# Decode attention over 65,536 keys: the first piece of keys issued in two halves of partitions, by SyncE and by ScalarE

## The chip, the core and the metric

The kernel runs on one core of a Trainium2 chip. The metric is the device time of one execution in microseconds; lower is better. Engines are called PE (TensorE), DVE (VectorE), ACT (ScalarE), POOL (GpSimd) and SP (SyncE). SP and ACT can issue transfers; each has a queue of its own (q1 for SP, q10 for ACT in the profile), and both feed the same 16 DMA engines.

## The reference

One query token attends over a long cache, with 32 query heads and 8 key/value heads, all in bfloat16:

```python
B, Hq, Hkv, Sq, Sk, D = 1, 32, 8, 1, 65536, 128
k = jnp.repeat(k, rep, axis=1)          # rep = Hq // Hkv = 4
v = jnp.repeat(v, rep, axis=1)
scores = jnp.einsum("bhqd,bhkd->bhqk", q, k) * D ** -0.5
p = softmax(scores, axis=-1)
return jnp.einsum("bhqk,bhkd->bhqd", p, v)
```

The keys and the values of one key/value head are 16.8 MB each, so 268.4 MB are read in all; the output is 8 KB.

## The kernel before

**Tiling.** There are G = 8 groups (one key/value head with its H = 4 query heads). A group's 65,536 keys are laid out as 128 partitions with 512 keys each (`kr[g]`, `vr[g]`), and handled in two halves of NT = 256 keys per partition. Such a half is a tile: 128 partitions x 64 KiB, 8.4 MB. `buf` holds three tiles, used in a ring. A piece of a tile is loaded by `load(at, src, s, lo, n)` (L134), always for all 128 partitions, from `lo` for `n` keys.

**Order of transfers.** SP issues every load of keys and values, in a fixed order `tiles`: both key tiles of group 0, then of group 1, then values and keys of later groups in turn. The first four loads are half tiles of keys (128 partitions x 32 KiB, 4.2 MB); the first of them is issued as SP's very first instruction, ahead of the barrier that opens the program (`tc.close()`, `tc.compile()`, L147 in the profile), the other three right behind that barrier, and then the first tile of group 1. From then on, SP waits before each load until the tile three places earlier has been used up: for keys on `clr` (the bank clears of the scores) or `kb`, for values on `vit`. The last value tile is cut into eight `PIECES`, the smallest at the end, so that little work is left when the last bytes arrive.

**Semaphores of the keys.** `sK[b][x]` counts the landing of half x in ring place b, by 16 for each load. `take` waits for a count and takes it off again.

**Work of the engines.** DVE first builds small selection matrices, waits for q on `sQ` and transposes it (L310). q (32 x 256 bytes) is ACT's first transfer (L227), issued behind the barrier. Then DVE loops over the groups, in blocks with branches (`keys`, `keys0`, `keys1`, `keys2`, `turned`). `turn(b)` takes `sK[b][x]` for both halves of a tile and transposes the keys in place (L320). PE takes `kt` and multiplies the turned keys into `sc`, one bank for each half tile (`bank`, `scores`, L465). ACT does the exponentials (L244), DVE the maxima and the transposes of the weights, and PE accumulates the weighted values of the group before into `psum_o` (`values`, L489). Between PE's query product (L446) and the first scores, ACT casts the spread query into `qx` (L229) and POOL multiplies it into the sliding weights `wq` (L208).

**The tail.** For the last value tile, PE waits for the pieces one by one (L542, L554), DVE picks from `psum_o` (L333), ACT scales and stores. In DVE's block `last`, a few `nop` instructions count up `dl`, ahead of `dve.wait_ge(vdone, 2)` and behind it.

At the end POOL clears all semaphores in `cleared`, which is the list of those allocated up to that line.

Of the kernel before, what the change touches and what calls it, by code (L numbers as in the profile page):

```python
# [15 lines left out]
P = 128  # L16
D = 128
NT = 256
# [14 lines left out]
def kernel(  # L33
# [18 lines left out]
    _, Hkv, Sk, _ = k.shape  # L52
# [5 lines left out]
    pe, dve, act, pool, sp = nc.tensor, nc.vector, nc.scalar, nc.gpsimd, nc.sync  # L58
    half = NT * D
    ring = 3 * half  # L60

    def sbuf(name, shape, dtype=fp32):
        return nc.alloc_sbuf_tensor(name, list(shape), dtype)
# [4 lines left out]
    buf = sbuf("buf", (P, ring), bf16)  # L68
# [27 lines left out]
    def sem(name):  # L96
        sems.append(nc.alloc_semaphore(name))
        return sems[-1]

    sK = [[sem(f"sK{b}{x}") for x in range(2)] for b in range(3)]  # L100
    sC, sD = sem("sC"), sem("sD")
    sL = [sem(f"sL{x}") for x in range(sum(map(len, BY.values())))]
    sP = [sem(f"sP{x}") for x in range(len(PIECES))]
    sQ = sem("sQ")
    sV = sem("sV")
    kt = sem("kt")
    clr = sem("clr")
# [21 lines left out]
    kr = [k[0, g].rearrange("(p n) d -> p (n d)", p=P) for g in range(G)]  # L129
    vr = [v[0, g].rearrange("(p n) d -> p (n d)", p=P) for g in range(G)]  # L130

    def load(at, src, s, lo=0, n=NT):
        at = at % 3 * half + lo * D
        return sp.dma_start(  # L134
            out=buf[:, at:at + n * D], in_=src[:, s * half + lo * D:s * half + (lo + n) * D]
        )

    first = load(0, kr[0], 0, 0, NT // 2)  # L140
    tc.no_tile_sem_insts.add(first.ins.name)
    first.then_inc(sK[0][0], 16)
    tc.add_to_no_dep_group("first", first.ins)
    tc.declare_fence(pool.nop().ins, group="first")
    home = nc.cur_bb.parent
    tc.close()
# [11 lines left out]
    for at, (kind, h, s) in enumerate(tiles):  # L158
# [35 lines left out]
        out=ident[:, :], in_=ident[:, :], compare_op=ALU.not_equal, fill=1.0,  # L194
# [8 lines left out]
    for g in range(G):  # L203
        if g == 0:
            pool.wait_ge(qxs, 1)
        else:
            pool.wait_ge(outs, g)
        pool.tensor_tensor(  # L208
            out=wv[:, :, :, 0:H],
# [12 lines left out]
    def take(engine, semaphore, n=1):  # L222
# [7 lines left out]
        out=qx[:, :].rearrange("p (b r h) -> p b h r", b=2, r=2),  # L230
        in_=misc[:, 0:P].rearrange("p (b h r) -> p b h r", b=2, r=2),
# [9 lines left out]
    for g in range(G + 1):  # L241
        if g < G:
            act.wait_ge(nms, g + 1)
            act.activation(  # L244
                out=E[:, :], in_=sc[:, :], func=ACT.Exp, bias=nmb[:, 0:1], scale=SCALE,
# [4 lines left out]
        at = max(g - 1, 0) * D  # L250
        act.activation(  # L251
            out=o_out[:, at:at + D], in_=psum_f[0:H, 0:D], func=ACT.Copy, scale=rl
# [12 lines left out]
        out=o_out[:, 0:D], in_=misc[0:H, 0:D], func=ACT.Copy, scale=rl_next  # L265
# [5 lines left out]
    def value(reg, below):  # L271
        return bass.RuntimeValue.of_register_unchecked(reg, min_val=0, max_val=below - 1)

    def moved(ap, by):

        return bass.AP(ap.tensor, ap.offset + by, ap.ap)
# [7 lines left out]
    def select(out, pattern, **at):  # L284
# [7 lines left out]
        out=rep.rearrange("p (a x) -> p a x", a=4),  # L292
        in_=ident[0:32, 0:32].unsqueeze(1).broadcast_to([32, 4, 32]),
# [6 lines left out]
        out=rows4[:, :].rearrange("k (y d) -> k y d", y=4),  # L300
        in_=ident[0:4, 0:4].unsqueeze(2).broadcast_to([4, 4, D]),
# [3 lines left out]
        out=away.rearrange("k (q z r h) -> k z q r h", q=4, z=2, r=4)[:, 0],  # L305
# [5 lines left out]
        out=qt.bitcast(fp32), in_=qn.bitcast(fp32)  # L311
# [10 lines left out]
    def weights(s):  # L322

        at = slice(1024 * s, 1024 * (s + 1))
        return dve.transpose(out=Ew[:, at], in_=E[:, at])  # L325

    def next_over():

        return dve.tensor_copy(out=rl, in_=rl_next)  # L329

    def picked():

        return dve.tensor_reduce(  # L333
            out=o_r[:, 0:D], in_=psum_o[:, :].rearrange("p (y d) -> p d y", y=4), axis=AX.X, op=ALU.max
        )

    def over():

        dve.reciprocal(out=rl_next, in_=psum_f[0:H, D:D + 1]).then_inc(rls, 1)  # L339
# [6 lines left out]
    r_h, r_k = dve.alloc_register("h"), dve.alloc_register("k")  # L346
    h, kb_at = value(r_h, G + 1), value(r_k, 3)
    dve.reg_mov(r_h, 0)
    dve.br("keys")

    with block("keys"):
# [15 lines left out]
    with block("turned"):  # L367
# [8 lines left out]
            out=same[:, :].rearrange("p (x h) -> p x h", h=H),  # L376
# [11 lines left out]
    with block("last"):  # L388
        dve.wait_ge(exd, 1)
        dve.wait_ge(vit, NT // STEP * (2 * G - 3))  # L390
        weights(0)
        dve.wait_ge(vdone, 1)
        next_over().then_inc(mxs, 1)
        picked().then_inc(mxs, 1)
        weights(1).then_inc(sP[0], 16)
        dve.wait_ge(pes, 2)
        over()


        for _ in range(6):  # L400
            dve.nop().then_inc(dl, 1)
        dve.wait_ge(vdone, 2)
        picked().then_inc(mxs, 1)
        for _ in range(5):
            dve.nop().then_inc(dl, 1)
        dve.nop().then_inc(fin, 1)
        dve.br("done")
# [22 lines left out]
    def column(row):  # L430

        return 4 * (row // W * W + W - 1 - row % W)
# [26 lines left out]
    with block("scores"):  # L459
# [3 lines left out]
        for y in range(4 * N):  # L463
            m, n = y % 4, y // 4
            pe.matmul(  # L465
                out=bank,
# [17 lines left out]
    with block("values"):  # L484
        take(pe, sV)
        weight = value(r_w, 2048 - 127)
        rows = value(r_p, ring - STEP * D + 1)
        for j in range(STEP // 4):
            last = pe.matmul(  # L489
                out=psum_o[0:16, :], lhsT=moved(Ew[:, column(4 * j + 3):][:, 0:16], weight),  # L490
# [14 lines left out]
    with block("summed"):  # L505
# [4 lines left out]
            out=misc[:, :], lhsT=same[:, :], rhs=each[:, :].unsqueeze(1).broadcast_to([P, 16, 32]),  # L510
# [22 lines left out]
    with block("tail"):  # L533
        at = sum(PIECES[:MOVED])
# [3 lines left out]
        for n, land in left[:1]:  # L538
            pe.wait_ge(land, 16)
            for row in range(at, at + n, 4):  # L540
                qd = row // 4 % 4 * 32
                pe.matmul(  # L542
                    out=psum_o[qd:qd + 16, :], lhsT=Ew[:, final + column(row + 3):][:, 0:16],
# [4 lines left out]
        for y, (n, land) in enumerate(left[1:]):  # L548
# [4 lines left out]
            for row in range(at, at + n):  # L553
                last = pe.matmul(  # L554
                    out=misc[0:H, 0:D], lhsT=Ew[:, final + column(row):][:, 0:H],
# [43 lines left out]
```

## Time and profile before

| what | value |
|---|---|
| median of 3 runs | 627.47 us (627.43 to 627.98) |
| the profiled execution | 628.09 us |
| its span, first to last instruction | 626.2 us |
| granted TensorE clock, mean | 0.926 |
| bytes read | 268.44 MB, 429 GB/s over the span |
| busy: PE, DVE, ACT, POOL | 80%, 53%, 3%, 1% |
| time of q1's packets, share of 16 DMA engines | 99.4% |
| first key load issued | 0.73 us |
| DVE's first turn of keys | 12.88 us |

How to read it: times in the profile are microseconds from the start of the span. A busy share says how much of the span an engine worked. A DMA share of 1.0 in a stretch means that all 16 DMA engines had a packet under way all the time; a packet is counted where it starts, so in short stretches the share and the GB/s swing above and below. A name like `SPq` or `DVEq` is the engine's own sequencer: waits and issues that are not compute. In a line of the stretches, the columns are the stretch, its length, busy time of PE, PEld, DVE, ACT and POOL with the number of instructions, the granted clock, the DMA share and GB/s.

### The profile page before, as it was taken

The page shows a single profiled execution, that of the slowest core. Times are in us where ns is not written, and L with a number is a line of the kernel's source. Part 1 is how long each engine was busy: PE and PEld are TensorE (multiplying, and loading weights), DVE is VectorE, ACT ScalarE, POOL GpSimd, SP SyncE. Part 2 cuts the span into 40 slices and gives each one's busy share as a digit, 9 for nine tenths or more (in the row PEclk, how much of TensorE's full clock was granted, in tenths as well). Part 3 has the DMA queues.
Part 4 walks back from the last instruction along what each step waited for, and adds up shares of the span by engine and source line. Part 5 has one row for each costly group of instructions (what it writes and reads, how often), then busy time and mean ns, then how long its engine had stood idle before and what let it go on. Part 6 is the DMA issues. An engine that isn't in the chain of part 4 may idle for free. (4 is left out here: it accounts for less than half of the span.)

```text
span 626.2 us, 8002 instructions
## 1 busy us (share of the span) xinstructions
PE 501.8 (80%) x2186; PEld 203.8 (33%) x2186; DVE 331.1 (53%) x109; ACT 21.1 (3%) x28; POOL 6.0 (1%) x16
## 2 busy tenths in 40 slices
PE   0587398798995879948799397993979939899998
PEld 0233043243331333313333133331433314333433
DVE  4984894689213892148921488215872169621010
ACT  1000100100010000100001000010000100001000
POOL 2000000000000000000000000000000000000000
PEclk9989599798998789987999779997889978999999
DMA  9999999999999999999999999999999999999998
GB/s 371 435 467 402 419 452 402 469 402 469 402 469 402 469 402 469 402 469 402 469 402 460 410 427 444 402 469 402 469 402 469 402 435 435 469 402 433 425 415 336
DMA packets 6425, 268.46 MB, mean 429 GB/s; under 512 B 792, under 2 KB 1048, under 8 KB 1176
## 3 DMA queue, kind: packets, MB, share of 16 engines
q1 hardware_dynamic: 6336, 268.44, 99.4%
q10 hardware_dynamic: 88, 0.02, 0.0%
q14 instruction: 1, 0.01, 0.0%
HBM read 268.44 MB, written 0.01 MB: 429 GB/s over the span
## 5 line engine op out<-in xcount | busy, mean ns | idle before, releaser
L320 DVE STREAM_TRANSPOSE buf<-buf 128x8192 f32<-128x8192 f32 x32 | 276.9, 8691 | 95.9 <-DVEq L224 95.9
L465 PE MATMUL sc<-buf,zeros 128*128 x1024 | 247.6, 401 | 0.0
L489 PE MATMUL psum_o<-buf,Ew 128*16 x1008 | 224.0, 380 | 6.6 <-PEq L224 6.6
L465 PEld LDWEIGHTS sc<-buf,zeros 128*128 x1024 | 102.3, 100 | 137.4 <-issue 39.1
L489 PEld LDWEIGHTS psum_o<-buf,Ew 128*16 x1008 | 88.8, 88 | 138.1 <-issue 48.5
L423 PE MATMUL sc<-zeros 128*128 128x512 bf16 x32 | 14.0, 439 | 96.5 <-PEq L224 96.5
L333 DVE TENSOR_REDUCE o_r<-psum_o 128x128 f32<-128x512 f32 x10 | 6.9, 688 | 94.6 <-DVEq L224 69.1
L329 DVE COPY o_r<-o_r 4x1 f32<-4x1 f32 x9 | 1.3, 142 | 77.2 <-DVEq L224 64.2
L423 PEld LDWEIGHTS sc<-zeros 128*128 128x128 bf16 x32 | 3.1, 98 | 105.6 <-issue 104.4
L244 ACT ACTIVATE zeros<-sc,nmb 128x2048 bf16<-128x2048 f32 x8 | 15.7, 1967 | 539.8 <-DVE nmb L384 539.8
L325 DVE STREAM_TRANSPOSE Ew<-zeros 128x1024 bf16<-128x1024 bf16 x18 | 22.3, 1239 | 13.8 <-PE psum_o L489 13.8
L509 PE MATMUL misc<-each,same 128*128 128x512 f32 x18 | 11.4, 720 | 8.3 <-PEq L224 8.3
L372 DVE TENSOR_REDUCE mx<-sc 128x1 f32<-128x2048 f32 x8 | 18.0, 2252 | 0.0
L446 PE MATMUL misc<-Ew 32*128 32x128 bf16 x1 | 0.3, 283 | 10.6 <-DVE Ew L310 10.6
L208 POOL TENSOR_TENSOR zeros<-qx,quad 128x64 bf16<-128x64 bf16 x8 | 2.3, 292 | 486.8 <-ACT o_out L251 480.7
L509 PEld LDWEIGHTS misc<-each,same 128*128 128x128 f32 x18 | 2.9, 201 | 8.6 <-issue 8.5
L426 PE MATMUL sc<-zeros 128*128 128x1 bf16 x32 | 5.2, 163 | 0.0
L423 PE MATMUL psum_o<-rows,zeros 4*128 4x512 bf16 x10 | 4.5, 452 | 0.0
L291 DVE CAST Ew<-ident 32x128 bf16<-32x128 f32 x1 | 3.0, 2984 | 2.7 <-POOL ident L193 2.7
L426 PEld LDWEIGHTS sc<-zeros 128*128 128x128 bf16 x32 | 3.0, 95 | 3.9
L251 ACT ACTIVATE o_out<-psum_f,o_r 4x128 bf16<-4x128 f32 x9 | 3.1, 344 | 27.9 <-DVE o_r L339 27.9
L436 PE MATMUL psum_f<-o_r,sel 128*4 128x129 f32 x18 | 3.9, 302 | 0.0
(32 smaller groups left out, 32.0 us busy)
## 6 DMA issues: line engine op xcount, KB each, us to landing
buf<-in_k_dram SPq DMA_DIRECT2D x6, 4096.0 KB, 28.4
buf<-in_v_dram SPq DMA_DIRECT2D x4, 4096.0 KB, 31.8
buf<-in_v_dram SPq DMA_DIRECT2D x2, 2048.0 KB, 30.0
buf<-in_v_dram SPq DMA_DIRECT2D x2, 1024.0 KB, 35.2
buf<-in_v_dram SPq DMA_DIRECT2D x1, 1408.0 KB, 39.2
buf<-in_v_dram SPq DMA_DIRECT2D x1, 288.0 KB, 39.4
buf<-in_v_dram SPq DMA_DIRECT2D x1, 224.0 KB, 39.6
buf<-in_k_dram SPq DMA_DIRECT2D x13, 32.5
```

Source lines behind the costliest of these rows:

```text
L244: act.activation(out=E[:, :], in_=sc[:, :], func=ACT.Exp, bias=nmb[:, 0:1], scale=SCALE, accum_out=o_r[:, D:D + 1],).then_inc(exd, 1)
L251: act.activation(out=o_out[:, at:at + D], in_=psum_f[0:H, 0:D], func=ACT.Copy, scale=rl).then_inc(outs, 1)
L320: dve.transpose(out=kv, in_=kv).then_inc(kt, 1)
L325: return dve.transpose(out=Ew[:, at], in_=E[:, at])
L333: return dve.tensor_reduce(out=o_r[:, 0:D], in_=psum_o[:, :].rearrange("p (y d) -> p d y", y=4), axis=AX.X, op=ALU.max)
L372: after(dve.tensor_reduce(out=mx[:, :], in_=sc[:, :], axis=AX.X, op=ALU.max))
L423: return pe.matmul(out=bank, lhsT=lhsT, rhs=rhs, start=True, stop=False)
L426: return pe.matmul(out=bank[:, 0:1], lhsT=zer[:, 0:P], rhs=zer[:, 0:1], start=False, stop=True)
L436: return pe.matmul(out=out[0:H, 0:n], lhsT=sel[:, :], rhs=o_r[:, 0:n], start=start, stop=stop)
L465: pe.matmul(out=bank, lhsT=moved(wq[:, m * SLIDE + 4 * n:][:, 0:P], slide), rhs=moved(T[:, n, m // 2, m % 2], keys), start=False, stop=False,)
L489: last = pe.matmul(out=psum_o[0:16, :], lhsT=moved(Ew[:, column(4 * j + 3):][:, 0:16], weight), rhs=moved(buf[:, 4 * j * D:][:, 0:4 * D], ...
L509: pe.matmul(out=misc[:, :], lhsT=same[:, :], rhs=each[:, :].unsqueeze(1).broadcast_to([P, 16, 32]), start=True, stop=True,).then_inc(pes, 1)
```

## The change

The first half tile of keys is no longer one transfer of 128 partitions issued by SP. SP issues partitions 0 to 63 of it and ACT partitions 64 to 127, each as the first instruction of its engine, ahead of the barrier. SP's half counts on `sK[0][0]` as before, ACT's on a new semaphore `sF`. DVE waits for `sF` once, behind the transpose of q and before the loop over the groups. One `nop` of DVE in the block `last` is dropped. ACT's transfer of q now stands behind ACT's half of the keys in q10. All other transfers are issued as before.

```diff
-    sQ = sem("sQ")
+    sQ, sF = sem("sQ"), sem("sF")
...
-    first = load(0, kr[0], 0, 0, NT // 2)
-    tc.no_tile_sem_insts.add(first.ins.name)
-    first.then_inc(sK[0][0], 16)
-    tc.add_to_no_dep_group("first", first.ins)
+    for engine, at, land in ((sp, 0, sK[0][0]), (act, P // 2, sF)):
+        rows = slice(at, at + P // 2)
+        first = engine.dma_start(out=buf[rows, 0:half // 2], in_=kr[0][rows, 0:half // 2])
+        tc.no_tile_sem_insts.add(first.ins.name)
+        first.then_inc(land, 16)
+        tc.add_to_no_dep_group("first", first.ins)
     tc.declare_fence(pool.nop().ins, group="first")
...
     dve.reg_mov(r_h, 0)
+    dve.wait_ge(sF, 16)
     dve.br("keys")
...
-        for _ in range(6):
+        for _ in range(5):
             dve.nop().then_inc(dl, 1)
         dve.wait_ge(vdone, 2)
```

## Prediction

> **What bounds the kernel now.** I read the page first: busy times, DMA line, queues, chain.
>
> ```profile
> PE 501.8 (80%) x2186; PEld 203.8 (33%) x2186; DVE 331.1 (53%) x109; ACT 21.1 (3%) x28; POOL 6.0 (1%) x16
> ...
> DMA  9999999999999999999999999999999999999998
> ...
> q1 hardware_dynamic: 6336, 268.44, 99.4%
> q10 hardware_dynamic: 88, 0.02, 0.0%
> ```
>
> No engine is busy for more than 80% of the span, but SyncE's queue (q1) keeps the 16 DMA engines busy for 99.4% of it. 268.44 MB / (16 x 0.994 x 626.2 us) is 26.95 KB per us and DMA engine, so a row of 32 KiB takes about 1.216 us. The trace's packet records agree: 1280 packets of 32 KiB with a median of 1.214 us. Next, the busy time by stretches, to see whether the transfers ever pause (last columns: DMA share, GB/s):
>
> ```profile
> 1.50:1.75 0.25, 0.00 (x0) 0.00 (x0) 0.00 (x0) 0.00 (x0) 0.00 (x0) 1.00 0.96 262
> 1.75:2.00 0.25, 0.00 (x0) 0.00 (x0) 0.00 (x0) 0.00 (x0) 0.11 (x1) 1.00 5.04 1442
> 2.00:2.25 0.25, 0.00 (x0) 0.00 (x0) 0.00 (x0) 0.00 (x0) 0.10 (x1) 1.00 1.22 393
> ```
>
> ```profile
> 100.00:200.00 100.00, 86.55 (x377) 35.09 (x375) 49.83 (x22) 4.60 (x6) 0.59 (x2) 0.95 1.02 440
> 200.00:300.00 100.00, 78.69 (x335) 32.13 (x336) 60.99 (x15) 2.30 (x3) 0.29 (x1) 0.88 0.99 430
> 500.00:600.00 100.00, 86.04 (x380) 34.67 (x378) 43.61 (x17) 2.66 (x4) 0.00 (x0) 0.95 1.00 430
> ```
>
> The first lines count a packet's bytes where it starts: 2, 11 and 3 rows of 32 KiB, one for each DMA engine, between 1.731 and 2.222 us by the records. After that there is no pause: a share of about 1.0 at 430 to 440 GB/s. The chain of waits ends the same way:
>
> ```profile
> 583.03 39.16 DMA buf<-in_v_dram
> 622.19 0.04 issue
> 622.24 0.82 PE psum_o L542 x11
> ```
>
> The last pieces sit 39 us in the queue; behind this landing come 4.0 us of the smallest pieces, TensorE, ScalarE and the store. So the time is the start of the stream, plus bytes over rate, plus that tail. A change to the first piece counts only if it moves the stream's start or its rate; a slow first piece is not made good later, because no later stretch has spare rate.
>
> **The change part by part.** The profiled execution took 628.09 us, of which 626.2 are the span and 1.9 lie around it. The median of the runs is 627.47, so 0.62 comes off each sum.
>
> *Start of the stream.* SyncE issues the piece at 0.73 us, and the first packets start 1.0 us later, spread over 0.49 us. ScalarE leaves the same barrier (0.652 us against SyncE's 0.647), so both halves are issued together. With half the rows to each queue the spread may halve. Bounds: 0 to -0.25 us; I take -0.2.
>
> *Issue on ScalarE.* One more issue, by its issue of q, 0.40 us at 1.90. SyncE's takes 0.37 at the same moment, and the barrier that follows waits for both: at most 0.1 us on everything after it. SyncE's next load, at 1.88 us, is covered by 9.7 us of queued rows, and the table load that follows q by the 7.31 us that ScalarE idles before its cast at 10.93. Nothing on the path.
>
> *q behind the keys.* q is moved past nothing in program order, but now stands behind four rows per DMA engine in ScalarE's own queue.
>
> ```profile
> Ew<-in_q_dram ACTq DMA_DIRECT2D x1, 8.0 KB, 8.4
> buf<-in_k_dram SPq DMA_DIRECT2D x1, 58.4
> ```
>
> ```profile
> 10.32 0.23 DVE L310 STREAM_TRANSPOSE Ew<-Ew 32x64 f32<-32x64 f32 x1 [4.31 <-DMA Ew<-in_q_dram]
> 12.88 8.71 DVE L320 STREAM_TRANSPOSE buf<-buf 128x8192 f32<-128x8192 f32 x1 [2.33 <-DVEq L224]
> 22.57 8.71 DVE L320 STREAM_TRANSPOSE buf<-buf 128x8192 f32<-128x8192 f32 x1 [0.98 <-DVEq L224]
> 32.28 8.71 DVE L320 STREAM_TRANSPOSE buf<-buf 128x8192 f32<-128x8192 f32 x1 [1.00 <-DVEq L224]
> ```
>
> In the packet records the two queues take turns, a row of keys and then one packet of q. With q behind the piece, its two rows and its count each wait for one row of the next load: 3 x 1.21 = 3.6 us after the piece, which ended at 12.37. VectorE transposes q first, so its first turn starts at about 16.7 instead of 12.88. It idles about 1.0 us before each later turn, so four turns give that back. The work that opens the next buffer is the start of bank 2's scores: 41.29 us before, some 2 us later now. The last load queued ahead of it was issued at 3.28 and landed 58.4 us later, at 61.7, so 20 us of rows are still queued. Cost 0; without that cover up to 3.8 us.
>
> *The wait on sF.* It stands on VectorE before the first turn; queued behind it are all its transposes. Both halves are needed anyway: 0. The dropped nop lies in a 25.5 us idle time of VectorE (its wait for psum_o before the last pick): 0.
>
> *The rate of the first piece.* This is the disputed term, and no transfer before shows it: every large one spans 128 partitions. There each DMA engine gets 8 rows. Now it gets 4 rows in partitions 0 to 63 and 4 in 64 to 127, in turns. If all 16 stand in the lower half at once, they write into half of the partitions. The nearest rows are these same rows of keys, 1.213 us each, and they give both bounds. If 27 GB/s is what a DMA engine can do, the piece takes 8 x 1.213 = 9.7 us as before: +0. If it is what a sixteenth of the partitions can take, two DMA engines share one and each row takes 2 x 1.213: +9.7 us, all of it on the path. A gain is excluded, as the share is already 1.0.
>
> I take a value near the upper bound, for two reasons. First, the rate hardly depends on anything at the source or in the packet: 8, 16, 32 and 64 KiB packets take 0.313, 0.615, 1.214 and 2.421 us, keys or values, with VectorE and TensorE busy or idle. This looks like a path of fixed width, and the destination is the part of it that the change halves. Second, the DMA engines keep their step: their rows start within 0.43 us of each other at 3.4 us, at 11.9 and at 22.8. So those that begin together in the lower half also change to the upper half together. A pair that is d apart loses 8 x (1.213 - d); one d of 0.06 takes 0.5 off. The slowest DMA engine counts, as all carry equal shares of every load. So +9.2.
>
> [...]
>
> Sum: 628.09 - 0.2 + 9.2 = 637.1 for a profiled execution, 636.5 as a median.
>
> **Rivals.**
> - *No rate loss.* The limit is the DMA engine's own, or those that share a place happen to stand in opposite halves. 628.09 - 0.2 - 0.62 = 627.3. For it: before, a DMA engine and its 8 partitions can't be told apart, and ScalarE's and SyncE's first rows arrive within about 0.01 us, so some may start with one half and some with the other. Against it: one pair in step is enough for the whole loss.
> - *Partial loss.* All pairs are some way out of step, 0.6 us each: 8 x 0.6 = 4.9 us, near 632. The 0.43 us spread speaks against so much.
> - *Faster by over 0.2%.* The mechanism is a quicker start. The first packets took 1.5 to 2.06 us instead of 1.21; if two queues hid all of that excess (about 0.6 us) and the full 0.25 of spread, the gain is 0.85: 626.6. To pass 0.2% another 0.4 us is needed, which only an issue before 0.73 us would bring, and ScalarE leaves its barrier at 0.652.
> - *The change doesn't do what it says.* ScalarE's half could come late, as q's first packet did (issued at 1.90, started at 5.85). Then SyncE's half and next load go first. The DMA engines stay busy, so this is 627.4 or, with the loss in each half in turn, again 636.5. It lies within the cases above.
>
> **How the numbers follow.** 0.2% is 1.25 us; three runs spread over 0.55 us, so that is about what a measurement of this kernel can tell from no change. Chances: rate halved, or nearly, 0.57; partial loss 0.08; no rate loss 0.30; faster by over 0.2% 0.05. I put the halved rate at about two to one over no loss, for the two reasons above and because one pair decides. Its own range is 633.5 (pairs 0.4 us apart) to 637.5 (none of the terms that take off). As no loss holds 0.30, the range must take it in: from 627.0 (its start gain and run spread) to 637.6. Slower is 0.57 + 0.08 = 0.65, same 0.30, faster 0.05.
>
> **What would show it.** By the packet records or the stretches after: between 2 and 22 us about 220 to 240 GB/s if I am right, about 430 if not, with 32 KiB packets near 2.4 us or 1.2. VectorE's first turn near 25.5 us (21.6 for the piece, 3.6 for q, 0.3 for its transpose) or near 16.7. The later stretches at 430 to 440 GB/s as before, the last landing about 9 us later, and the 4.0 us tail unchanged. I am wrong if the first piece lands near 12.4 us, or if it lands late and the end doesn't move.

## The result and the profile after

| | before | after |
|---|---|---|
| median of 5 runs | 627.56 us (627.43 to 627.98) | 637.23 us (637.19 to 637.51) |
| ratio of the times | | 1.0153 (95%: 1.0142 to 1.0164) |
| profiled execution, its span | 628.09, 626.2 us | 637.23, 635.4 us |

The change makes the kernel 9.67 us slower. The page of the changed kernel, its 40 slices and its queues:

```profile
DMA  9999999999999999999999999999999999999998
GB/s 200 353 435 464 396 462 396 462 425 433 462 396 462 396 462 408 450 454 404 462 396 462 400 458 450 408 462 396 462 400 458 441 413 466 396 462 396 429 430 331
...
q1 hardware_dynamic: 6272, 266.34, 97.9%
q10 hardware_dynamic: 168, 2.11, 1.5%
```

ScalarE's queue now carries 2.11 MB, half of the first piece: the change does what it says. The DMA line still shows 9 up to the last slice, as before, and the packets of the two queues take 97.9% and 1.5% of the 16 engines' span, so the DMA engines had packets under way nearly all the time. Only the GB/s of the first two slices (0 to 31.8 us) tell of the loss: 200 and 353, where before they were 371 and 435:

```profile
GB/s 371 435 467 402 419 452 402 469 402 469 402 469 402 469 402 469 402 469 402 469 402 460 410 427 444 402 469 402 469 402 469 402 435 435 469 402 433 425 415 336
```

The stretches (columns as before; last two: DMA share, GB/s) separate the piece from the rest. The first line is the kernel before, the others the changed kernel:

```profile
2.00:20.00 18.00, 0.71 (x2) 0.12 (x2) 10.70 (x8) 2.01 (x2) 3.63 (x5) 1.00 0.97 414
...
4.00:20.00 16.00, 0.00 (x0) 0.00 (x0) 2.65 (x6) 0.24 (x1) 2.21 (x2) 1.00 1.05 227
100.00:200.00 100.00, 93.11 (x413) 38.44 (x411) 59.92 (x22) 4.60 (x6) 0.58 (x2) 0.97 0.99 430
500.00:600.00 100.00, 86.67 (x382) 35.02 (x382) 42.51 (x16) 4.60 (x6) 0.29 (x1) 0.93 1.00 430
```

A busy share of 1.05 at 227 GB/s, against 0.97 at 414 before, means that each packet takes about twice as long. By the packet records (the profile's list of every packet with its queue, start and duration), the 32 KiB rows of the piece take 2.36 us where the halves alternate and 2.55 to 2.56 where the same half follows itself; before, they took 1.21. The very first rows stand apart: they took 1.5 to 2.06 us before and take 1.73 to 2.81 now. The first row of the next load takes 1.43 to 2.08, the later ones 1.21 to 1.23 again. The end has moved with the stream, as the chain of waits shows:

```profile
592.18 39.17 DMA buf<-in_v_dram
631.35 0.04 issue
631.39 0.82 PE psum_o L545 x11
```

The landing is at 631.35 instead of 622.19; the 39.17 us in the queue and the 4.0 us behind the landing are as before. VectorE's start is much later, as its timeline shows:

```profile
27.51 0.23 DVE L312 STREAM_TRANSPOSE Ew<-Ew 32x64 f32<-32x64 f32 x1 [20.86 <-DMA Ew<-in_q_dram]
28.36 34.49 DVE L322 STREAM_TRANSPOSE buf<-buf 128x8192 f32<-128x8192 f32 x4 [0.62 <-DVEq L226]
```

The first turn begins 15.5 us later, 6 us more than the stream has lost. The four turns then run without a gap, and no load is late because of it.

**One reading for all runs.** The records name no DMA engine, but the rows start in groups of 16 (before the change within 0.43 us of each other), which I take as one for each. Counted so, the tenth row of each starts at 13.15 to 13.58 us before the change and at 22.75 to 23.33 after it: 9.67 us later (mean of both ends), which is the whole difference of the medians. (The two profiles differ by only 9.14, since the profiled execution of before lost about 0.5 us later in its stream, between 41 and 81 us, and lies that much above its median.) The same reading for the experiments, with the extra time of their medians; the rows are medians of a group, without the first row of the piece and, in e4 and e7, without the first slow one (2.1 us), and in e2 two rows of 16 KiB count as one:

| run | rows of the first piece, us | tenth row later by | median minus before |
|---|---|---|---|
| after | 2.36 (half changes), 2.56 (same half) | 9.67 | 9.67 |
| e1_one_queue | 2.56; 2.40 at the one change | 10.61 | 10.58 |
| e2_two_queues_full | 0.61 (16 KiB rows) | 0.14 | 0.02 |
| e3_quarters | 2.56; 2.41 where the half changes | 10.34 | 10.32 |
| e4_middle | 1.21 to 1.24, then 2.37 to 2.55 | 5.69 | 5.59 |
| e5_source_rows | 2.40, 2.55 | 9.88 | 9.82 |
| e7_source_middle | 1.21 to 1.24, then 2.37 to 2.55 | 5.73 | 5.59 |
| e8_every_other | 1.21 | 0.49 | 0.34 |
| e9_every_eighth | 2.54; 2.35 at one change | 10.61 | 10.67 |
| e10_sixteens | 4.47 | 26.08 | 26.07 |

Except for e6_two_pieces (below), what the first piece loses arrives unshortened at the end.

### The profile page after: what moved, and what is told of

Read it like the earlier page. It is cut to its first block, busy times and chain, and to the rows that moved or that the text cites. A ratio compares the mean times of both kernels' runs of the same rounds, so it can differ in the third digit from the quotient of the medians.

```text
span 635.4 us, 8003 instructions
## 1 busy us (share of the span) xinstructions
PE 500.1 (79%) x2186; PEld 203.4 (32%) x2186; DVE 330.7 (52%) x109; ACT 21.1 (3%) x28; POOL 6.0 (1%) x16
## 3 DMA queue, kind: packets, MB, share of 16 engines
q1 hardware_dynamic: 6272, 266.34, 97.9%
q10 hardware_dynamic: 168, 2.11, 1.5%
```

## The experiments

All start from the changed kernel and differ in how the first piece is issued. Each median stands beside that of the kernel before on the same chip.

**Is it the queues, the halves or the late q?** e1_one_queue:

```diff
-    for engine, at, land in ((sp, 0, sK[0][0]), (act, P // 2, sF)):
+    for engine, at, land in ((sp, 0, sK[0][0]), (sp, P // 2, sF)):
```

> Both halves of 64 partitions are issued by SyncE, one after the other; ScalarE issues q alone, as before. Theory H (a transfer whose 16 DMA engines all stand in one half of the partitions runs at half rate): 8 rows of about 2.36 us per DMA engine instead of 1.21, so the same loss without the later start: 636.5 to 637.0 us. Rival Q (two queues that take turns cost the rate): one queue, so no loss, 627.5 to 628. Rival L (the late first turn of VectorE, caused by q behind the keys): q lands early again but the piece itself stays slow under H; under L alone about 628.

Measured: 638.09 us, ratio 1.0168 (1.0151 to 1.0185). One queue has the full loss, and 0.9 us more than two, as the halves change only once and four rows more take 2.56 instead of 2.36 us. Q falls, and H's figure was 1.1 us too low for the same reason.

e2_two_queues_full:

```diff
-        rows = slice(at, at + P // 2)
-        first = engine.dma_start(out=buf[rows, 0:half // 2], in_=kr[0][rows, 0:half // 2])
+        cols = slice(at, at + half // 4)
+        first = engine.dma_start(out=buf[:, cols], in_=kr[0][:, cols])
```

with `at` 0 for SyncE and `half // 4` for ScalarE.

> SyncE and ScalarE each issue half of the piece at the same time, but each for all 128 partitions and half of the columns (16 KiB rows). H: full rate, so only the later start of the stream seen after the change (first packets at 2.05 to 2.95 us instead of 1.73 to 2.22) is left: 627.8 to 628.4 us. Q: the two queues still take turns, so the loss stays: about 637. L: q is again behind the keys in ScalarE's queue and VectorE's first turn is some 3.8 us late; if a late turn costs, 630 to 632.

Measured: 627.53 us against 627.51, ratio 1.0001 (0.9991 to 1.0011). Two queues, taking turns row by row, run at full rate (16 KiB rows of 0.61 us): this stretch is from that run.

```profile
8.00:12.00 4.00, 0.00 (x0) 0.00 (x0) 0.00 (x0) 0.00 (x0) 0.00 (x0) 1.00 1.02 438
```

Its VectorE also starts late, at no cost in time:

```profile
16.52 0.23 DVE L312 STREAM_TRANSPOSE Ew<-Ew 32x64 f32<-32x64 f32 x1 [10.52 <-DMA Ew<-in_q_dram]
17.38 34.49 DVE L322 STREAM_TRANSPOSE buf<-buf 128x8192 f32<-128x8192 f32 x4 [0.62 <-DVEq L226]
```

So L falls too, at this size: a first turn 4.5 us late is covered. The later start that H expected did not come either; the first packets started at 1.74 to 2.51 us.

**How does the rate go with the partitions?** e3_quarters and e4_middle, both by SyncE alone (`sF` is waited for with 16 for each transfer on it):

```diff
+    for at, land in ((0, sK[0][0]), (32, sF), (64, sF), (96, sF)):           # e3
+        rows = slice(at, at + 32)
...
+    for at, n, land in ((32, 64, sK[0][0]), (0, 32, sF), (96, 32, sF)):       # e4
+        rows = slice(at, at + n)
```

> The piece as four transfers of 32 partitions, all by SyncE. If the rate goes with the number of partitions (H in its plain form), a row takes 4 x 1.21 us: 8 x 3.64 = 29 us more, about 656 us. [...] Under Q about 628.

> SyncE issues partitions 32 to 95 as one transfer, then 0 to 31 and 96 to 127. If any 64 neighbouring partitions run at half rate, the first four rows of a DMA engine cost 4 x 1.15 us more and the two quarters at least as much: 637 us or above. [...] Under Q about 628.

Measured: e3 637.83 us (ratio 1.0164, 1.0147 to 1.0181), e4 633.10 (1.0087, 1.0070 to 1.0104). A quarter is no slower than a half (a row takes 2.55 to 2.56 us in both), and 64 partitions in the middle are not slow at all: in e4 the first transfer and the two quarters behind it show side by side.

```profile
4.00:7.60 3.60, 0.00 (x0) 0.00 (x0) 3.32 (x6) 0.93 (x1) 2.88 (x2) 1.00 0.96 410
...
10.00:16.00 6.00, 0.71 (x2) 0.13 (x2) 0.23 (x1) 0.73 (x1) 0.29 (x1) 1.00 1.04 218
```

So the number of partitions alone does not set the rate: rows of 2.36 to 2.56 us in the halves of 64 (after), 1.21 to 1.24 in the 64 in the middle (e4). In e3 rows are faster (2.41 us) where partitions 32 to 63 are followed by 64 to 95, but not where 0 to 31 are followed by 32 to 63 (2.55): a change between the first two quarters gains nothing, just as a half that follows itself (2.56).

**Source or destination?** e5_source_rows and e7_source_middle change only what is read:

```diff
-        first = engine.dma_start(out=buf[rows, 0:half // 2], in_=kr[0][rows, 0:half // 2])
+        first = engine.dma_start(out=buf[rows, 0:half // 2], in_=kr[0][at // 64::2, 0:half // 2])   # e5
...
+    for at, of, n, land in ((32, 0, 64, sK[0][0]), (0, 64, 32, sF), (96, 96, 32, sF)):             # e7
+        rows, read = slice(at, at + n), slice(of, of + n)
```

> The changed kernel with other source rows: the lower 64 partitions read the even rows of the keys, the upper 64 the odd rows, so each half spreads over the whole source (the keys land in other partitions than the values belong to; the output is another one). [...] Rival S (64 neighbouring rows of the source are the limit): the loss goes, 627.5 to 628.5.

> As the run with partitions 32 to 95 first, but these read rows 0 to 63 of the keys, partitions 0 to 31 rows 64 to 95 (so the output is another one). [...] S: rows 0 to 63 are the slow set wherever they land, so all eight rows are slow: 637 to 638.

Measured: e5 637.44 us (ratio 1.0155, 1.0138 to 1.0172), e7 633.21 (1.0089, 1.0073 to 1.0106). Each has the time of the run with the same destinations, 637.23 and 633.10, and its rate. This is e5; before the change, the stretch from 2 to 20 us ran at 414 GB/s:

```profile
8.00:20.00 12.00, 0.00 (x0) 0.00 (x0) 0.00 (x0) 0.00 (x0) 0.00 (x0) 1.00 1.01 218
```

S falls: with the same destinations the time stays within 0.21 us (e5) and 0.11 (e7), so the loss goes with where the rows are written.

**Does the loss repeat?** e6_two_pieces issues the second half tile in the same way, and VectorE waits for `sF` with 32:

```diff
-    load(0, kr[0], 0, NT // 2, NT // 2).then_inc(sK[0][1], 16)
+    for engine, at, land in ((sp, 0, sK[0][1]), (act, P // 2, sF)):
+        rows = slice(at, at + P // 2)
+        engine.dma_start(
+            out=buf[rows, half // 2:half], in_=kr[0][rows, half // 2:half]
+        ).then_inc(land, 16)
```

> The second piece of keys is also issued in two halves of partitions by SyncE and ScalarE. [...] If the loss belongs to the start of the queues and not to the halves: 637 to 638. If VectorE's first turn, now waiting for both pieces (about 41 us), were no longer covered by the loads queued behind: over 648.

Measured: 654.89 us, ratio 1.0433 (1.0416 to 1.0451). The loss repeats: behind the second piece the stream is 19.5 us late. The other 7.8 of the 27.3 us are the last case, a late VectorE. Its stretches:

```profile
100.00:110.00 10.00, 2.31 (x6) 0.90 (x7) 10.00 (x2) 0.31 (x2) 0.29 (x1) 0.50 0.97 419
110.00:120.00 10.00, 10.00 (x46) 4.33 (x44) 10.00 (x2) 0.00 (x0) 0.00 (x0) 0.94 0.73 315
120.00:130.00 10.00, 9.03 (x42) 3.92 (x41) 10.00 (x2) 0.00 (x0) 0.00 (x0) 1.00 0.55 210
```

The DMA share falls to 0.73 and 0.55 while VectorE is busy throughout. The first turn began at 47.91 us, so the load that waits for group 1's first key tile to be used is issued at 125.3 us instead of 93.2, and from 119.2 to 126.3 us no row is under way. The cover that the prediction named is real and ends here: a first turn that lags 6 us behind the stream's own delay costs nothing (after), one that lags 15.5 us behind it (35.0 less 19.5) costs about 8.

**Two halves, or something finer?** e8_every_other, e9_every_eighth and e10_sixteens:

```diff
-        rows = slice(at, at + P // 2)
+        rows = slice(at // 64, P, 2)          # e8, SyncE and ScalarE
...
+    for at in range(8):                       # e9 and e10, SyncE alone
+        land = sF if at else sK[0][0]
+        rows = slice(at, P, 8)                # e9
+        rows = slice(16 * at, 16 * at + 16)   # e10
```

> The changed kernel with SyncE taking every even partition and ScalarE every odd one. [...]

> The piece as eight transfers of 16 partitions, all by SyncE, each with every eighth partition (one row per DMA engine and transfer). [...] Theory 2 (two halves, partitions 0 to 63 and 64 to 127, each with half of the rate, and nothing finer): both halves are written evenly, rows of 1.21 us, 627.5 to 629 us with the eight issues.

> The piece as eight transfers of 16 neighbouring partitions, all by SyncE. [...] Theory 2: a block lies in one half, rows of 2.56 us, 637.5 to 639 us.

Measured: e8 627.96 us (ratio 1.0007, 0.9998 to 1.0017), e9 638.22 (1.0169, 1.0152 to 1.0186), e10 653.62 (1.0417, 1.0400 to 1.0435). Taken alone, e8 looked like theory 2. But e9 is slow (2.54 us a row) although it writes both halves evenly, and a row of e10 takes nearly twice as long as one of a half (4.47 us against 2.56) although each block lies in one half. These are e8, e9 and e10, in this order:

```profile
8.00:20.00 12.00, 0.71 (x2) 0.12 (x2) 1.21 (x2) 0.73 (x1) 0.29 (x1) 1.00 0.97 418
...
8.00:20.00 12.00, 0.71 (x2) 0.13 (x2) 3.13 (x7) 1.15 (x2) 2.46 (x2) 1.00 0.99 206
...
10.00:20.00 10.00, 0.00 (x0) 0.00 (x0) 0.00 (x0) 0.00 (x0) 0.00 (x0) 1.00 1.22 142
20.00:30.00 10.00, 0.71 (x2) 0.13 (x2) 0.23 (x1) 0.73 (x1) 0.29 (x1) 1.00 0.90 105
```

With 16 rows in a transfer, taken as one for each DMA engine, the order within a transfer cannot matter, so theory 2 falls: e9 has 638.22 us where it expected 627.5 to 629, e10 653.62 where it expected 637.5 to 639. A limit that is shared within smaller sets of partitions than a half would fit both. An estimate from the row times, in units of one row per 1.213 us: 16 rows in 2.54 to 2.56 us (e9, e3) go at a rate of 7.6 (each row takes 2.1 x 1.213), 16 rows in 4.47 us (e10) at 4.3 (3.7 x 1.213). How many such sets there are, and which partitions belong to one, no run shows. The eight issues are not what makes e10 slower than e9, as both have eight. In both, source and destination change together; that it is the destination is shown for the halves and the middle alone (e5, e7).

Why then is e8 fast? Two single runs, both by SyncE alone: e11 is e8 in one queue, e12 is e3 with every fourth partition (`rows = slice(at // 32, P, 4)`).

> Every even partition, then every odd one, both by SyncE alone. The run with two queues had rows of 1.21 us. If it was the turns of the two queues that kept the DMA engines in different places, one queue gives rows of 2.4 to 2.6 us and about 637.5 us. If it is the way the rows of such a transfer are dealt to the DMA engines, rows stay at 1.21 us and the time at 627.5 to 628.5 us.

> Four transfers of every fourth partition, all by SyncE, two rows per DMA engine and transfer. [...]

Measured: 627.99 and 627.83 us, with a single run of 627.83 for the kernel before beside both; rows of 1.21 to 1.25 us behind the first. The turns of the two queues are not the reason, as e11 has only one queue. Why steps of 2 and 4 partitions keep the rate while a step of 8 does not (2.54 us, e9) stays open: how the rows of a transfer are dealt to the DMA engines is not shown, as the packet records name no DMA engine.

No version is faster than the kernel before; e2 equals it, and e8 can't be told from it.

## Why the prediction was right

The range says little for it: from 627.0 to 637.6 it took in no loss as well. The part of it for the halved rate, 633.5 to 637.5, comes out of its own terms as 633.8 to 637.2. What bears the prediction out is the mechanism.

*The rate of the first piece* (+9.2) is what happened, and what the first reason took for likely is now shown: the loss goes with the destination (637.44 us in e5 against 637.23, 633.21 in e7 against 633.10). That 27 GB/s is what a sixteenth of the partitions can take, the condition of the upper bound, was my supposition and no run shows it; the runs showed rows of 2.55 to 2.56 us in a half or a quarter that follows itself, 2.54 in every eighth partition, 4.47 in 16 neighbouring ones and 1.21 to 1.24 in the 64 in the middle. The second reason was half right. The DMA engines don't all stay in step: the 16 starts of a row lie 1.2 us apart in the piece, where before it was 0.43. Yet nearly the full loss came; why it did with the starts so far apart is not shown. A row takes 2.56 us where a half follows itself, not 2 x 1.213 = 2.43, and each change of halves gives back about 0.2 us, not 0.06. The two errors cancel to the 2.36 us of the alternating rows (predicted: 2.43 - 0.06 = 2.37). Nor did eight rows lose 1.15 us each: by the mean durations the first lost 0.4, five alternating ones 1.15 each, the two where a half follows itself 1.3 each, and the first row of the next load 0.5. That this adds up to 9.2 is in part luck.

*Start of the stream* (-0.2) had the wrong sign. The first packets started at 2.05 to 2.95 us instead of 1.73 to 2.22, 0.3 to 0.7 later. ScalarE's sharing is not the cause: SyncE alone with 64 partitions (e1) took 0.54 us for the issue and started at 2.06 to 2.96, and both engines with 128 partitions (e2) took 0.37 and 0.40 and started at 1.74 to 2.51. In these runs it goes with the shape of the transfer.

*Issue on ScalarE* (at most 0.1 us behind it) was mis-sized: SyncE's next load came at 2.53 us instead of 1.88. This too goes with the shape, as e2, in which both engines issue, had it at 1.89. It cost nothing, as argued, since rows were queued until 21.9 us.

*q behind the keys* cost 0, as predicted, but came later than worked out: first turn at 28.36 us, not 25.5. The order behind the piece is ScalarE's last row of keys, a row of the next load, ScalarE's count, a row, q, a row, q, a row, q's count: four rows, not three. The first of them is slow too (1.43 to 2.08 us), while other DMA engines still write their last row of the piece. VectorE then idled 0.62 us before the turn. (For a piece without loss the prediction gave 16.7, which its own terms, 12.37 + 3.6 + 0.3, make 16.3; e2 measured 17.38.)

*The sum* gave +9.0 us and 9.67 were measured. The gap is the start: by the same reading as for the tenth row (mean of both ends), the first rows start 0.52 us later instead of 0.2 sooner, and the rows between cost the other 9.15. Of the rivals, no rate loss needed DMA engines in opposite halves; all 16 began with SyncE's half, as their first two packets in q1 show. Partial loss is what e4 shows (5.59 us), with half of the rows slow; faster never came near.

## What to carry to other kernels

Where transfers are the limit, as here, time a split by where its rows are written, not by how many engines issue it: in this kernel two halves of the partitions cost 9.67 us from two queues and 10.58 from one (e1), while two halves of the columns, each over all 128 partitions, cost 0.02 from two queues (e2). The busy share of the DMA engines did not show the loss (1.05 in the slow piece, 0.97 before), the GB/s (227 against 414) and the duration of a packet (2.36 to 2.56 us against 1.21) did. In this stream, which has no pauses, the start of a later row is a direct reading of the end: the tenth row matched the medians within 0.15 us in every run but the one in which the queue ran dry. The two single runs agree less well: the tenth row came 0.59 us (e11) and 0.47 (e12) later, the time 0.16 and 0.00 above the one run of before.

## What the runs showed of the hardware that was not expected

- The issue of the first transfer goes with its partitions in these runs: 0.37 us for 128, 0.38 for the first 32 or 16 neighbouring ones, but 0.54 to 0.60 for 64, for every fourth or for every eighth one; the first packet then starts at about 2.05 to 2.12 us instead of 1.73 to 1.77. The same partitions can also take longer behind another transfer: 0 to 31 took 0.38 us first in e3, but 0.56 behind 64 others in e4.
- Rows written to one half of the partitions, or to a quarter, run a little below half rate (2.55 to 2.56 us against 1.213), rows written to 16 neighbouring partitions a little above a quarter of it (4.47).
- Every second or every fourth partition keeps the full rate (rows of 1.21 to 1.25 us behind the first), every eighth does not (2.54).
